# A recurrence and an MLP on one core: another string for the order of all steps

## The chip, the cores and the metric

The kernel runs on one core of one Trainium2 chip. A core has a matrix engine (TensorE, in profiles PE, with its weight loads as PEld), three engines for elementwise work (VectorE or DVE, ScalarE or ACT, GpSimd or POOL), and SyncE (SP), whose queue issues all of this kernel's DMA transfers in order. Every engine works through its own list of instructions in order, and waits with semaphores for the results of others. The metric is the time of one execution on the device in microseconds (us); it is given as the median of a few runs.

## The reference

Two blocks follow each other. The first is a recurrence with a complex decay; per batch and head (4 x 8), over 768 tokens, with states of 48 x 48:

```python
mag = np.sqrt(a_re * a_re + a_im * a_im)
scale = np.minimum(mag, 0.999) / (mag + 1e-06)
a_re_n, a_im_n = (a_re * scale, a_im * scale)
...
for t in range(S):
    ar, ai = (a_re_n[:, :, t, :, None], a_im_n[:, :, t, :, None])
    new_re = ar * S_re - ai * S_im
    new_im = ar * S_im + ai * S_re
    kv = np.einsum('bhd,bhe->bhde', k[:, :, t], v[:, :, t])
    S_re, S_im = (new_re + kv, new_im)
    y[:, :, t] = np.einsum('bhd,bhde->bhe', q[:, :, t], S_re)
```

Its output, laid out as 3072 tokens of 384 numbers, goes through an MLP with 2048 features:

```python
h = x @ w_in
g = np.maximum(h, 0.0) + alpha * np.minimum(h, 0.0)
return (g @ w_out).astype(np.float32)
```

The two weight arrays come in as 64-bit floats.

## The kernel before

The kernel is written as a set of Python generators ("tasks"). Each `yield` in a task ends a *step*; what stands behind a `yield` issues the instructions of that step, as a rule one to a few on one engine. A list of tasks is built, and a string decides which task makes its next step: one letter per step, 4292 letters in all.

```python
    def run(self, order):
        for c in order:
            next(self.tasks[self.LETTERS.index(c)], None)
```

So the string sets, for each engine and for SP's DMA queue, in which order the instructions of the tasks stand. Semaphore waits follow from the data. `Ring.put`, `takes=` and the numbers in the calls `DVE(...)`, `ACT(...)`, `PE(...)`, `DMA(...)` have no effect here: those calls return `None` and the body of `Ring.put` is `pass`. They are left from a planner that isn't part of the kernel.

The tasks and their letters:

- `A` to `I`, `gates`: the nine pieces of the decay, over one to three chunks of 128 tokens of a batch (`A`: batch 0, chunk 0; `B`: chunks 1 and 2; `C`: chunks 3 to 5; `D` to `I`: two halves for each of the other batches). A piece loads a_re and a_im (L248), makes magnitudes and phases on ACT and DVE (L253 to L311; the first DVE sum is L260), multiplies decays in a tree (L319) and writes them to the DRAM array `decs` (L324). It makes running products of phases with small products (L339, L341, on DVE where they are large, on POOL where they are small; in piece `A` all on DVE), carries them over the blocks (L379 to L414), and writes the phases to the DRAM array `phs` (L422, L432) after the products L427 and L430. The tile `gate` has two buffers, so a piece's loads wait for the end of the piece before the last.
- `J`, `loads`: per unit of 128 tokens the loads of queries and keys (tile `KQ`, L578, L580), phases (`PP`, L586) and decays (`T`, two transfers, L593).
- `K`, `half_rows`: copies rows of v to a DRAM array `vsc` (L561). `L`, `loads_v`: loads of v (`V`, L602 to L607, and `VL`, L625, L628).
- `M`, `pieces`: loads of `alpha` and of the 16 pieces of both weights (L492). `N` and `O`, `weights`: turn each piece into 32-bit floats in `to_f32` (L508, L510, L512 on ACT, L516 on POOL, L518 and L520 on DVE) for `w_in` and `w_out`.
- `P` to `Z` and `a` to `m`, `unit`: the 24 units (4 batches of 6 chunks) of the recurrence. A unit turns q and k by the phases (DVE L662, L664), then halves the distance of tokens level by level, 1 to 32: decay products on DVE (L718), copies on ACT (`WQ` L741, `W` L757), score products on PE (`ps_lv`, L679), masks on DVE or ACT (L703, L700). It then transposes k (PE L786, ACT L788, L789), makes the sum of the chunk's state (PE `ps_kv` L798, DVE `St` L827, L830, first set up with L723 and L726), the output (`ps_y`, PE L809, L818, L842), and stores it to DRAM (ACT L856, DMA L861). The state of a unit feeds the next unit of the batch.
- `n`, `loads_x`: loads the outputs of one or two units as `xT` (L874).
- `o`, `all_mlp`: the MLP over 14 groups of one or two units. A *feature* (16 in each group, 224 in all) is three products `ps_h` on PE (L890), a Relu on ACT (L897) and a DVE instruction (L899) that writes `g_sb`; then come the products `ps_o` of a unit with one feature (PE L909), 16 of them added up, a copy (ACT L919) and the store of 128 rows of the output (L922).

PE is needed by the units and by the MLP, and the MLP of a group can't start before its units have ended. DVE is needed by gates, weights, units and MLP.

Of the kernel before, what the change touches and what calls it, by code (L numbers as in the profile page):

```python
# [30 lines left out]
    "AAAAAAAAAAAAAAAAAAAAAAAAAAMMMAAMMJBBBBAMBJNNNNAAAAAAAAAAAAABABNANAAAAAABAAAABBABBNNAABBMBBABBNAAAABB"  # L31
    "BBBKBAAKKBJNABAKBAKAKAKAKOKNKJKKKKAAAAKOBBBANAABKABOMAABMAAAAABABAAABAAOOOOOOOBNNOOBBNOONNBNMNNNBJJB"
    "BBBBOPJPONPPPPPNMNPPOOPOOOPPCCLLMMMLLLLBLLJBCBBBPBBBBBBBJJBBBBBBBBBBBBBPPPPPPNOBCCCPCPPPBBNKCKKKKKCK"
    "LLKLBBBBBOBLLPPPPPPPPBBBBBBBPCCCCCLCBBNCCJBBBBPPPOBOOOOCPPPPBCMJDDCCNCCOCOCPCJCNCOOCJJJCOCONNNNCCCPD"
    "DKCQCCCCCDDNCLLLLCQDCCQCCCCCCCCCCCOQLNLPPPPPPMQMQQQQPPPPJQQLODDQQQODJJOJJJJJJQQQDDQCQCCDCCQDCQRKCOKL"
    "CLLLLLLKnRRRQRQRQQQQQQQQQQRQRQQRCCCCCQCQCRCNNNDDCDDoDQooDoooLLLoooQoDMoLQooCDDDCoRCoCoCDoooooNRoNNCo"
    "CoKNCCCCLLLRRRoooooLLLLLLDRLRRQQCCCCCCCRKKRMKCCRRoQCDooCQQQQRRoRRQCCoooooCoCoDDDRRRRRRRRRRoDoRJORoDR"
    "oDOOOOODRJJEJNDoooooLLDRRRRoRRRRDoSoOooSDSooDLoooJoLLooSSDSEoooSJooDooonoSSoDoSSDNNNSLLENoDoSSSoooLN"
    "DLooooSDooRSSSEJoJooOOoooooSSSoJLESoTESSSSLoLLLoTSJoooJSSSJooJSoJJooooSSSSSSooDESSEKTKESSESSSSSSDSoo"
    "UDUooTTTDoDTDoDDDDDDKooDDDDoooooooTDTTTLEoEToooELLTTTTTooooLoooJoJoTTooooEoUTTTTTTTTooooooUUTToUTTLT"  # L40
    "EELLLLLLLLDDDDDDEEEDDDDDDDDLoooDDDDDDoTooTTTTooTLnLLLEEoooEUULLLLLLLKoTooooooEoLUEoooLoToDDUoTDooDUo"
    "DDDDooooooooUEoEEUUoEEEDTToTTTTTooToUoUoUoooUooDUooooDooooUUUUUUUUUoooooDDDUoDooUoUUooooEUUUUUUoDoEo"
    "oEoEoooJUJUUUUUEUEJEEJJoooooEJEoEJooooEoEooEUooEooEoooooVoooooooJEoVooVoVoooooVFFJJJooooUVJVVVFoEEoE"
    "EooEoEEEEEEVEVEnooJJVVELEEEoooooooLVoWWVVooLoLoLLFFVoooVVoooVWoLoEoooLoEooVLoWEWWVWoVEoVVVVoEoWLWLWE"
    "WLooEoFLVVVEVLoooVJJoVEoooVEJEJJWEEEEEoEFVVVVVVoWWVVVWFFFooELELoEooWFFFFFoooooLoWWLLLLLLWLoEoooooLEo"
    "EEEEoEoELLLoWWVVVVVVVEWVWWooooEoEooooJJEJooWoXWWWEFJWWEooooooWWoooooWWWWWWWWXWLLLWWWWWWWXFFooWoLLooL"
    "LXXXXoXooooXXXoJJJooooGXooooLXoFFFoGXXXXooooLXXooFoFooFoXYXoFXGonooooJJooLLGoYXXXooooXXXoXXoFLoLLFFF"
    "FYFooFoXYFoXoGYYYFYXYooFFooJJooFYoYooooooFKoJooJXXXXYXXLXXXXXGXXXXooFoXFooooFGoGooFFFFFFFFFFJJFJYYYY"
    "FooooYooYYooZoZZZoFooLoFLLLLooLLFLLFGLooooLooYYYYYLYLYoZYZZZZoooooKKKYKYooYooYooJooFFYFGKFFGZGJJGYYY"
    "YYYYYYYYLooLLoLFGKGoYYYYYYoZoKZoKooooooJoFLoFLFGoFGFFFoFFoFFFFFFFFFFoLLLZZZZnLZZZLooLLKooooLFFooooZo"  # L50
    "FZZooFFZFZFFoFoFJJFoJooFoFFooZZZJZJZoFZooooZZooZZZZZZZZZZZZFLLLFoaZZZZZaoooooooooooJaJJooaoGoooaaaaa"
    "ooooaoooooaoooGaaaaaaaaoooobooooGJGooLGoGGJGGaaaaaaaJJaLLLaGoGoooGoLLLLbbbbHHooooooaoooLoabLooaGGooG"
    "aaaaaaGaGaGHbbbHbGbHKbKGJaJaaooooooGGboooooooaoaaaGGaGoJoobbbboooGbbGbGGGGoGGGbcoooooooooLooLobLLLbL"
    "LLHJLbLJLcbLbboobooocoHobooooHHHooocobbbooocccccobbooLcnooLooooJJJHbbHHHbobbbbooLoHLLLHGccLLoLLLLLGL"
    "LHoGoooHoGooJGooHGboooooGoocGccGcGbGGGGbbGcGcGcGoooobobbobGJoooGGGGooGGGccccGGGGcoocccooLdccocoooodc"
    "ococccccccccccbbooJJLLGGGGGGGJJJGJcodcHcLLGococcHGGGoGoGooooooooLLoLoLoodooooodHGGdHoGodddddKKooHLLL"
    "LoKooHoooodoooddddJodLHLHoHddooJooHooHooddHooonodddHdoodddddooooHHHHHHHooooddIIoooodHHoddddJdddJddLH"
    "JdHdedddHHddeJJJoJJJJJJHooooooooooeooHoooooeeeeeeHeoeooooofooeooooofeeoeffeooeoooLLoooooJeoeooooooLe"
    "oeeeeeeffooogHHHHHHfHHHHHHHHHHHHHfHHHHHHHgHeeeeLLLLLLLLLLIKoooooeooeefeeeeeeeKeeeeeKeeeeHHooHooooofo"
    "ooJoHHHHfHJLLoLfoLHHLLLLoooLLooLffJJffIoILofLoLfofooooogoooogfgffffgfggfoffooooogggIoffooooooHHHHHHo"  # L60
    "HoooofIKooHHooofffffKKfngfHHofggggIIooKKLooooLLLLLLggLLLLgoLHoooggggggggoffffoffffooHofggfgoooooooHo"
    "ooooJJogooooLoooooIIgoooIJIIIIJoJgJJgggggggggohooIggggoIIoooooooIohhoogLLLLJJhhJJJoohoooooohhoooIooh"
    "hooohohoooohooonohoioIohhhhhohooiihoooooooooooJohiihiooIihIhhhIIIIhLoohooooKhoooohhLLoLLLLLILLIoIIIh"
    "oooiiihihhhhhhhhhhhhhhhhLoLhioooIooooooLLLLLooioiiioooiioioooIoooooiJiiiJooJJJLJJIIIIIIooooojoIoIooo"
    "ooIooIooojjIIIoIIIIoLIIoIIoIiijiiiiioooooooLojjLoLLoioLooioiIIIIiIIIIIIiIIIIIiiILLjLLLLLLLLojjjoioiI"
    "iioooojojooooojjioiIooIIiIIIIoILoojjjjojoooiILjjojiiioLLIIIIIIIIoIioooonjjjjjjjjooooIooIIooIooIooIoo"
    "oojooooojjjjjjjjjjjjjjjJJJJJjooooooojoooooJJJJoooookkLkoooooookoJooooookkoookkoookkoLojokokoookkkkko"
# [34 lines left out]
def kernel(  # L102
# [83 lines left out]
    for h in (16, 32):  # L186
        by_row[h] = []
        for m in range(HC // h):
            t = next(column)
# [812 lines left out]
```

## Time and profile before

| what | value |
|---|---|
| time, median of 3 runs | 845.73 us (845.33 to 848.05) |
| span of the profiled execution (first to last instruction) | 837.2 us |
| time of the profiled execution beside its span | the page gives none; the median lies 8.5 us above the span |
| PE busy | 696.3 us (83%) |
| DVE busy | 648.1 us (77%) |
| ACT busy | 440.9 us (53%) |
| POOL busy | 245.1 us (29%) |
| moved by DMA | 130.91 MB, 156 GB/s in the mean |
| PE idle ahead of L890 / of L909 | 3.0 / 10.7 us |

How to read what follows. A span cut into slices shows each engine's busy share in tenths. A row of the waits names an instruction by engine, tile and line, what it waited for, the sum of those waits in us, how many there were, and the longest. A table of stretches gives for each stretch its length, then the busy time (and number of instructions) of PE, PEld, DVE, ACT and POOL, the clock granted to PE, the share of time in which the DMA engines were busy, and the GB/s they moved. Idle time of an engine costs nothing by itself; it counts where another engine waits for what comes late.

### The profile page before, as it was taken

How to read it: one execution, taken by the hardware profiler on the slowest of the kernel's cores; microseconds unless marked ns; L12 is line 12 of the kernel's file. 1: busy time of each engine (PE TensorE's matmuls, PEld its weight loads, DVE VectorE, ACT ScalarE, POOL GpSimd, SP SyncE). 2: the span in 40 equal slices, each digit the busy share in tenths (PEclk: the TensorE clock that was granted, in tenths of full speed). 3: DMA queues.
4: the chain of work that ended last, by engine and by line, in shares of the span. 5: the costliest groups of instructions: out<-in, count | busy, mean ns of one | idle time of the engine just before them, and what ended most of it. 6: DMA issues, size and time to landing. Idle time of an engine off the chain costs nothing.

```text
span 837.2 us, 26824 instructions
## 1 busy us (share of the span) xinstructions
PE 696.3 (83%) x11488; PEld 528.6 (63%) x11488; DVE 648.1 (77%) x953; ACT 440.9 (53%) x941; POOL 245.1 (29%) x352
## 2 busy tenths in 40 slices
PE   0002317768899999998999999999999999999998
PEld 0001316656777777776777777767777777777776
DVE  5988998989898998978998898796877856642112
ACT  7868876557645847473656544655443424232211
POOL 5376678817216400240134313500004300000000
PEclk9999757889999999999999999999999999999999
DMA  7695994696379468558854689457635493412100
GB/s 207 202 274 171 262 266 120 201 218 169 79 218 235 112 176 247 125 150 212 240 142 119 154 241 220 115 130 175 165 113 123 116 228 78 103 33 54 30 20 10
DMA packets 194174, 130.91 MB, mean 156 GB/s; under 512 B 74120, under 2 KB 185864, under 8 KB 194056
## 3 DMA queue, kind: packets, MB, share of 16 engines
q1 hardware_dynamic: 194056, 129.20, 58.7%
q8 instruction: 90, 1.47, 0.7%
q14 instruction: 28, 0.23, 0.1%
HBM read 100.82 MB, written 35.71 MB: 163 GB/s over the span
## 4 chain that ended last, share of the span: by engine, by line
PE 68%; DVE 12%; DMA 8%; ACT 5%; issue 3%; POOL 2%; SPq 2%; DVEq 0%; ACTq 0%; POOLq 0%
PE ps_h L890 27%; PE ps_o L909 26%; PE ps_lv L679 4%; PE ps_y L818 4%; DVE KQ L718 3%; PE ps_kv L798 3%; DMA T<-decs 3%; PE ps_y L842 2%; PE ps_kt L786 2%; DMA phs<-gate 2%; DVE gate L339 1%; DMA V<-in_v_dram 1%; DMA KQ<-in_k_dram 1%; DVE gate L341 1%; DMA St<-in_v_dram 1%
## 5 line engine op out<-in xcount | busy, mean ns | idle before, releaser
L890 PE MATMUL ps_h<-xT,w_in_sb 128*128 128x256 f32 (+1 forms) x1344 | 301.2, 356 | 3.0 <-issue 2.4
L909 PE MATMUL ps_o<-w_out_sb,g_sb 128*128 128x384 f32 x768 | 294.6, 497 | 10.7 <-DVE g_sb L899 8.3
L890 PEld LDWEIGHTS ps_h<-xT,w_in_sb 128*128 128x128 f32 x1344 | 234.1, 193 | 74.0 <-issue 4.3
L899 DVE SCALAR_TENSOR_TENSOR g_sb<-g_sb,al,ps_h 128x256 f32<-128x256 f32 (+1 forms) x224 | 97.5, 438 | 112.8 <-ACT g_sb L897 112.1
L909 PEld LDWEIGHTS ps_o<-w_out_sb,g_sb 128*128 128x128 f32 x768 | 137.7, 191 | 63.4 <-DVE g_sb L899 10.8
L718 DVE TENSOR_TENSOR KQ<-KQ,T 96x1024 f32<-96x1024 f32 x120 | 151.4, 1263 | 30.4 <-PE ps_lv L679 21.4
L897 ACT ACTIVATE g_sb<-ps_h 128x256 f32<-128x256 f32 (+1 forms) x224 | 78.7, 352 | 181.8 <-PE ps_h L890 181.1
L679 PE MATMUL ps_lv<-WQ 96*32 96x32 f32 x2304 | 34.5, 203 | 71.4 <-DVE WQ L662 55.1
L679 PEld LDWEIGHTS ps_lv<-WQ 96*32 96x32 f32 x2304 | 26.6, 115 | 93.1 <-DVE WQ L662 54.7
L339 POOL TENSOR_TENSOR gate<-gate 128x72 f32<-128x72 f32 (+1 forms) x56 | 40.0, 714 | 129.4 <-ACT gate L369 125.6
L741 ACT COPY WQ<-KQ 96x1024 f32<-96x1024 f32 x48 | 50.0, 1042 | 31.0 <-DVE KQ L718 30.7
L856 ACT COPY T<-ps_y 48x256 f32<-48x256 f32 x96 | 30.6, 365 | 46.8 <-PE ps_y L842 46.2
L757 ACT COPY W<-KQ 96x512 f32<-96x512 f32 x48 | 30.6, 638 | 45.7 <-DVE KQ L718 35.5
L516 POOL TENSOR_SCALAR top<-top 128x768 f32<-128x768 f32 x16 | 39.3, 2461 | 25.1 <-ACT top L508 17.1
L339 DVE TENSOR_TENSOR gate<-gate 128x576 f32<-128x576 f32 (+3 forms) x70 | 45.7, 653 | 1.2
L319 POOL TENSOR_TENSOR gate<-gate 128x72 f32<-128x72 f32 (+5 forms) x24 | 22.3, 929 | 76.6 <-DVE gate L319 74.3
L818 PE MATMUL ps_y<-A,VL 64*48 64x64 f32 x2304 | 43.5, 228 | 1.0 <-DMA VL<-vsc 0.7
L427 DVE TENSOR_TENSOR gate<-gate 128x1152 f32<-128x1152 f32 (+2 forms) x36 | 42.8, 1219 | 1.6 <-POOL gate L412 1.5
L679 PE MATMUL ps_lv<-KQ,W 96*32 96x32 f32 x1536 | 24.6, 205 | 23.4 <-ACT W L757 23.3
L818 PEld LDWEIGHTS ps_y<-A,VL 64*48 64x48 f32 x2304 | 41.6, 129 | 1.6 <-DMA VL<-vsc 0.9
L700 ACT ACTIVATE A<-ps_lv,columns 128x64 f32<-128x64 f32 x144 | 36.5, 334 | 9.6 <-PE ps_lv L679 9.5
L703 DVE TENSOR_TENSOR A<-ps_lv,mask 128x256 f32<-128x256 f32 x96 | 36.8, 412 | 0.0
(105 smaller groups left out, 925.3 us busy)
## 6 DMA issues: line engine op xcount, KB each, us to landing
T<-decs SPq DMA_DIRECT2D x48, 384.0 KB
PP<-phs SPq DMA_DIRECT2D x24, 387.0 KB
KQ<-in_q_dram SPq DMA_DIRECT2D x48, 192.0 KB
decs<-gate SPq DMA_DIRECT2D x7, 1152.0 KB
phs<-gate SPq DMA_DIRECT2D x14, 576.0 KB
KQ<-in_k_dram SPq DMA_DIRECT2D x40, 192.0 KB
vsc<-in_v_dram SPq DMA_DIRECT2D x48, 144.0 KB
VL<-vsc SPq DMA_DIRECT2D x24, 288.0 KB
```

The source lines that it names most:

```text
L339: on(4 * k).tensor_tensor(out=m, in0=w[:, 1::-1].unsqueeze(2).to_broadcast([P, 2, 2, k]), in1=pairs_of(u), op=ALU.mult)
L427: TT(out=m[:, a], in0=U5[:, 1 + a], in1=turned(off3, o)[:, a].unsqueeze(1).unsqueeze(3).to_broadcast([P, L // 2, nb, 2]), op=ALU.mult)
L516: nc.gpsimd.tensor_scalar(out=top, in0=top, scalar1=F64_SMALL, scalar2=None, op0=ALU.max)
L679: nc.tensor.matmul(t[64 * i + j:64 * i + j + HC // 2, p], lhsT=keys(n, g), rhs=queries(n, g), start=True, stop=True)
L703: nc.vector.tensor_tensor(out=a.rearrange("p n (g t) -> p n g t", g=2), in0=t.unsqueeze(2).to_broadcast(whole), in1=masks[name].rearrange( ...
L718: nc.vector.tensor_tensor(out=x, in0=x if x0 is None else x0, in1=m, op=ALU.mult)
L741: nc.scalar.copy(z.rearrange("p i n t -> p i (n t)").rearrange("p i (m h) -> p m i h", h=h), bass.AP(tensor=KQ.tensor, offset=KQ.offset + ...
L818: nc.tensor.matmul(o, lhsT=Vp[h][64 * i:64 * i + 64, s, e_ * D:(e_ + 1) * D], rhs=a, start=False, stop=False)
L890: nc.tensor.matmul(p, lhsT=w_in_sb[:, f // 2, kk, f % 2 * P:(f % 2 + 1) * P], rhs=x_of[m][:, kk], start=(kk == 0), stop=(kk == NK - 1))
L897: nc.scalar.activation(gt, p, AF.Relu, scale=-1.0)
L899: nc.vector.scalar_tensor_tensor(out=gt, in0=gt, scalar=al_1[:, f:f + 1], in1=p, op0=ALU.mult, op1=ALU.add)
L909: nc.tensor.matmul(sums[0], lhsT=gt[:, c * P:(c + 1) * P], rhs=w_out_sb[:, f], start=(f == 0), stop=(f == NF - 1))
```

## The change

The string `ORDER` is replaced by another one of the same length with the same count of each letter. In `to_f32` a call `R["top"].put(t)` is added after the last step's instruction.

```diff
@@ ORDER
 ORDER = (
-    "AAAAAAAAAAAAAAAAAAAAAAAAAAMMMAAMMJBBBBAMBJNNNNAAAAAAAAAAAAABABNANAAAAAABAAAABBABBNNAABBMBBABBNAAAABB"
-    "BBBKBAAKKBJNABAKBAKAKAKAKOKNKJKKKKAAAAKOBBBANAABKABOMAABMAAAAABABAAABAAOOOOOOOBNNOOBBNOONNBNMNNNBJJB"
...
-    "ommmoooooooooooonooooooooooooooooooooooooooooooooooooooooooooooooooooooooooooooooooooooooooooooooooo"
+    "AAAAAAAABAAAAAABAMBMMABAAMAMAKBAAAJAAAAKAABANBBAABKAJMAKAAKANJAAAAAKANBAAABAABAABAAAAOAJABBMAABMABNOAA"
+    "NABKKKBKAAAKOOBBAAAAAAABBBBABLABAKKABAMNAALABOOAANAAAABAANNAAAOBNANBNBNMBBNNOOOBLBBBBBNBBBBCCBCCBBBC"
...
+    "Loooommmommmooooooomoooooooooommooooooooommooomoooooooooomoooomoooomooooonoooooooooooooooooooooooooooo"
@@ to_f32
         nc.vector._custom_dve(ADD32_U16LIMBS, out=halfwords(dst), in0=halfwords(top), in1=halfwords(dst))
         slots.append(slot)
+        R["top"].put(t)
         return t
```

Each engine gets the same instructions as before, each with the same shapes and the same data. Their order changes on every engine. The longest run of steps that stand in the same order in both lists (with others in between) is 1126 of 1417 on PE, 499 of 937 on DVE, 483 of 888 on ACT, 306 of 322 on POOL and 434 of 731 transfers in SP's queue. On PE the units and the MLP alternate in nearly the same way: by the end of unit 8, for instance, 202 of the 672 `ps_h` products and 84 of the 384 `ps_o` products stand ahead before, 201 and 84 after. Most of the difference lies inside: the third piece of the gates (`C`) starts earlier and the first MLP products stand earlier, some copies of `half_rows` stand later, the last piece of the gates (`I`) starts earlier, and steps of different tasks alternate more often.

## The prediction

> **What bounds the kernel now.** I read the slices of the page first, then a table of stretches, then the waits of VectorE (DVE) and TensorE (PE), because the change moves instructions and adds none: the question is which engine is full at which time.
>
> ```profile
> PE   0002317768899999998999999999999999999998
> DVE  5988998989898998978998898796877856642112
> POOL 5376678817216400240134313500004300000000
> PEclk9999757889999999999999999999999999999999
> DMA  7695994696379468558854689457635493412100
> ```
>
> PE is idle for three slices, limps for eight, and is full from the twelfth (about 230 us) to the end. DVE is the other way round: full from the second slice to about the 28th (580 us). The table of stretches, cut where the feature counts below need it, gives the same in microseconds; its columns are busy time of PE, PE's weight loads, DVE, ACT and POOL, then the granted clock, the DMA share and GB/s:
>
> ```profile
> 8.00:57.00 49.00, 0.66 (x32) 0.52 (x32) 43.68 (x105) 37.27 (x56) 23.47 (x27) 1.00 0.80 225
> 57.00:221.00 164.00, 89.62 (x2104) 72.43 (x2108) 149.38 (x192) 112.58 (x205) 102.47 (x106) 0.82 0.73 197
> 221.00:261.00 40.00, 39.76 (x570) 31.32 (x559) 37.70 (x61) 18.70 (x48) 11.77 (x19) 1.00 0.75 207
> 261.00:578.00 317.00, 311.76 (x5410) 233.99 (x5409) 277.87 (x376) 179.08 (x399) 83.38 (x145) 1.00 0.65 169
> 578.00:837.00 259.00, 254.45 (x3392) 190.29 (x3390) 138.66 (x218) 88.84 (x232) 17.36 (x38) 1.00 0.37 94
> ```
>
> So there are two stages. Up to 221 us DVE bounds (149.4 of 164 us busy in the second row) and PE waits for it. From 221 us PE bounds: 606.0 of 616.2 us busy (sum of the last three rows). What the first stage wastes is in DVE's waits between 57 and 221 us:
>
> ```profile
> DVE g_sb L899 <- ACT g_sb L897: 3.2, 4, 1.0
> DVE KQ L718 <- DMA T<-decs: 2.4, 2, 1.9
> DVE KQ L718 <- ACT top L508: 1.7, 1, 1.7
> DVE WQ L662 <- DMA V<-in_v_dram: 1.7, 1, 1.7
> DVE KQ L718 <- ACT WQ L741: 1.4, 4, 0.5
> DVE gate L427 <- POOL gate L412: 0.8, 1, 0.8
> ```
>
> With the smaller rows of that answer they are 13.2 us: that is all that a better order can take out there. In the second stage PE hardly waits for anybody (221 to 838 us):
>
> ```profile
> PE ps_h L890 <- issue: 2.4, 2, 1.3
> PE ps_o L909 <- issue: 2.2, 1, 2.2
> PE ps_y L818 <- DMA VL<-vsc: 0.7, 1, 0.7
> ```
>
> A new order can gain 6 us there at the very most, and can lose much more.
>
> **The change, part by part.** The call `R["top"].put(t)` runs a method whose body is `pass`: no instruction, nothing. The rest is the order. Every step issues the same instructions as before, so no duration changes; what changes is what stands ahead of what. I therefore counted, in both lists of instructions, the DVE work that stands ahead of a landmark: each instruction taken with the time that it added to DVE's busy time in this profile. PE work is counted by the mean durations after 250 us, where the clock is full (0.45 us for the two passes of a 256-column `ps_h` product, 0.67 us for the two of `ps_o`, and so on). The landmarks are MLP features (one `all_mlp` feature is three `ps_h` products, one Relu on ACT, one L899 on DVE), numbered from 0 to 223:
>
> ```
> feature  its L899 ended   DVE work before/after   PE work before/after
>    0        137.6 us        117.5 / 107.3            13.2 /   8.5
>   24        221.0           193.1 / 184.3            60.8 /  59.4
>   42        261.0           230.7 / 229.5           102.4 / 102.4
>   60        318.2           284.8 / 286.7           159.6 / 159.6
>  100        462.8           412.2 / 421.1           299.7 / 300.5
>  132        578.4           509.0 / 523.2           412.8 / 411.4
>  148        636.5           556.2 / 555.4           467.8 / 467.1
>  212        818.4           643.4 / 643.4           653.4 / 653.4
> ```
>
> The new order is the old plan with its details moved: at features 42, 60, 148 and 212 both engines have the same work behind them. So the time is decided by how fast feature 42 is reached, and whether PE is held up between 42 and 132.
>
> *First, features 24 to 42.* Feature 24 has 8.8 us less DVE work ahead of it (193.1 - 184.3). With the same DVE waits it comes at 212.2 us. From there DVE needs 45.2 us of work to feature 42 and PE 43.0. At the DVE density of 220 to 240 us (19.64 of 20 us busy, 0.98) that is 46.1 us: feature 42 at 258.3 us in place of 261.0, a gain of 2.7 us. At the 0.943 of the whole old stretch (37.70 of 40, where PE held DVE back) the gain is 0.9 us; with DVE full it is 3.6. I take -2.7, because DVE is the slower of the two now.
>
> *Second, DVE's waits up to 221 us.* Three stand in places that the order moves. The second T load of unit 3 has 0.89 MB less ahead of it in SP's queue (36.26 to 35.37 MB; 4.5 us at the 197 GB/s of that row), and unit 5's first products (L718) have 8.7 us more DVE work ahead while their T load has the same bytes ahead: the 2.4 us for T go. Unit 3's PP load has 1.03 MB less ahead, and its V load (L602, L604) 0.5 MB less: 1.7 us at L662 go. The Abs of `top` on ACT (L508) that ends unit 0's 1.7 us at L718 moves from just behind that unit's W copy to 26 ACT steps later, and this L718 gets 4.5 us more DVE work ahead: it goes. That is 5.8 us. What is new: the third gate chunk's loads move up, from behind PP, T and St of unit 0 in SP's queue to ahead of them (position 44 to 38), and its first DVE sum (L260) from 52.1 us of DVE work to 41.2, ahead of unit 0's second product (L664). Its 1.18 MB end at 10.09 MB in the queue; the old queue had moved 10.34 MB when PP landed, at 51.8 us, so they land about 51 us; ACT's L253 to L258 take 1.4 + 1.05 + 1.05 us, so the sum can start at about 54.5 us; DVE gets there at 41.2 plus the 11.5 us that it lags its work at that point (unit 0 starts at 51.8 us with 40.0 us done), 52.7. That is 1.8 us of new wait, with unit 0 queued behind it. The net is -4.0 us; the ends are -13.2 (all waits go) and +13.2 (as many come back elsewhere). I stay at what I can name.
>
> SP's transfers of the first unit come 0.15 MB (PP) and 0.59 MB (its second T) later by the same count, 0.7 and 2.6 us at 225 GB/s; St landed at 55.8 us and made DVE wait until then anyway, and DVE has 1.4 us more work ahead of the first L718, so I set this at nothing; uncovered it costs 1.2 us. The copies of V's rows (`half_rows`, L561) move down by up to 11 MB, off the loaded stretch; their unit comes after 170 us. On POOL 306 of its 322 steps keep their order; it made DVE wait 1.1 us before 221 us, and I leave that. SP gets 22 more separate waits; at the 17 ns that one took on ACT that is 0.4 us beside SP's own long waits, so nothing.
>
> *Third, features 42 to 132.* By feature 132 the new order has put 293.7 us of DVE work where the old one had 278.3, in the same 317.4 us of PE time: the gate work of the last chunk moves up by 44.6 us of DVE work, and the units of that stretch end with 6 to 22 us more ahead of them. DVE must be 0.925 busy or PE waits. The old order ran it at 0.877 there, held back by PE (of its waits the largest are for PE and for ACT behind PE). The nearest rows for what DVE can do are 55.85 of 59 us (261 to 320 us, 0.947: no loss) and 149.38 of 164 us (57 to 221 us, 0.911: 322.4 us, a loss of 5.0). I take the middle, +2.5; the ends are 0 and, at 0.877, +17.5. The work comes back by feature 148, but time that PE lost doesn't.
>
> *Last*, from feature 148 on the counts agree within 4 us on PE and DVE has slack: 0.
>
> Sum: -2.7 - 4.0 + 2.5 = -4.2 us on the profiled span of 837.2 us. The median of the runs, 845.7 us, lies 8.5 us above that span (the page has no total of its own); I carry the 8.5 over: 841.5 us.
>
> **The clock.** The PEclk row drops to 0.5 between 100 and 120 us, where PE was busy for 2.62 of 20 us, and stands at 1.00 from 220 us. PE was busy for 90.3 us before 221 us with work worth 60.8 at full clock, so 29.5 us went to the slow clock and its small products. I give it nothing, since DVE was the full engine then and waited only 3.6 us for PE or for ACT behind it. [...]
>
> **The rivals.**
> - *The first stage closes up.* All 13.2 us of DVE's waits go, since the gates come earlier and the MLP starts with 10 us less DVE work ahead of it: -2.7 - 13.2 + 2.5, so 832.3 us. For it: DVE and PE both have their work sooner. Against: 4.6 us of the waits are for ACT results that the same chains need in any order.
> - *DVE becomes the bound between features 42 and 132*, and it ends slower. Halfway between 0.877 and 0.90 of density, 0.888, DVE needs 330.7 us, PE loses 13.3 us: -6.7 + 13.3 = +6.6, so 852.3 us; at 0.877 it is 856.5. It decides from a density of 0.906 down, where the loss eats the 6.7 us. For it: no stretch of 300 us ran denser than 0.911. Against: the old density there was held down by PE.
> - *Nothing comes of it.* The waits that go come back as others and only -2.7 + 2.5 remain: 845.5 us.
>
> **How the numbers follow.** A measurement here tells about 0.3% (2.5 us) from no change. The forecast has 0.42, by itself 836 to 848 us, and of it 0.31 lies below 843.2, 0.09 inside 843.2 to 848.3 and 0.02 above. The closed first stage has 0.15, all faster. DVE as the bound has 0.30, all slower. Nothing has 0.13: 0.04 faster, 0.05 same, 0.04 slower. So 0.50 faster, 0.14 same, 0.36 slower. The range goes from 829 (the sum's low end, -3.6 - 13.2 + 0 = -16.8 us, is 828.9) to 858 (just past DVE at its old density); an order with new waits all over, up to -0.9 + 13.2 + 17.5 or 875 us, stays out.
>
> **What the profile would show.** If the steps are right: feature 42's L899 ends near 254 us in place of 261; the waits of L718 for T and of L662 for V before 221 us are gone; a wait of about 2 us stands at the third gate's L260 near 53 us; DVE's density between feature 42 and feature 132 is 0.91 to 0.95; and PE waits for L899 or for KQ a few us there. Wrong: PE waits of more than 7 us for DVE behind 260 us (the slower rival), a first MLP product after 137 us, or SP stuck on one wait with unit loads behind it.

## The result and the profile after

The changed kernel takes 851.15 us (median of 8 runs, 847.27 to 856.83) where the kernel before, run beside it, takes 844.9 (841.79 to 848.05). The ratio is 1.0083, 95% interval 1.0055 to 1.0111: slower by 0.8%. The forecast was 841.5 us, faster.

Executions of one kernel differ by some 10 us here: the profiled one of before (span 837.2 us) was among its quickest, that of after (span 855.1, 856.83 us with what lies around it) was the slowest of its eight, and the ratios below leave out two executions in a slower state (1097.13 us of h1_new_head, 858.10 us of the repeat of the changed kernel). Around the span lie 1.7 us, not 8.5. A second profile of the changed kernel, taken in a later experiment, has a span of 844.7 us, 846.45 us in all, below its median there. What both profiles of the changed kernel show is what I go by.

The slices of the changed kernel, to be laid against those of before; TensorE (PE), VectorE (DVE), GpSimd (POOL), PE's clock and the DMA engines:

```profile
PE   0001327669999998997999998999999999999998
DVE  5989988999998989699689986998655765534112
POOL 5369596353505710274078022413211000000000
PEclk9999857899999989999899999999999999999999
DMA  7695994787686469547566795486455474411110
```

PE has dips in slices 16, 19 and 25 (321 to 342, 385 to 406 and 513 to 534 us) where before had nines but for one 8 in slice 19. PEclk shows an 8 in slices 15 and 20 (299 to 321 and 406 to 428 us). The table of stretches has the same cuts and columns as before (busy time of PE, its weight loads, DVE, ACT, POOL; clock, DMA share, GB/s):

```profile
8.00:57.00 49.00, 0.66 (x32) 0.52 (x32) 42.21 (x103) 36.06 (x55) 22.78 (x30) 1.00 0.76 217
57.00:221.00 164.00, 88.85 (x1991) 69.78 (x1992) 151.39 (x198) 114.07 (x204) 104.94 (x109) 0.86 0.74 197
221.00:261.00 40.00, 37.64 (x673) 28.64 (x672) 37.07 (x57) 19.58 (x50) 5.09 (x5) 1.00 0.82 219
261.00:578.00 317.00, 301.64 (x5117) 224.89 (x5116) 275.65 (x370) 174.80 (x381) 121.21 (x156) 0.97 0.65 168
578.00:837.00 259.00, 258.64 (x3600) 194.44 (x3599) 136.50 (x213) 88.83 (x238) 18.16 (x34) 1.00 0.39 95
```

The first stage got better: DVE is 2.0 us busier from 57 to 221 us (151.39 for 149.38). The loss is in the fourth row: PE is busy for 301.64 of 317 us where it was 311.76, and at a clock of 0.97. DVE isn't full there either (275.65 of 317, 0.87). The ends of L899 (L900 in the changed kernel) say when, in us, before and then after: feature 24 221.0 and 212.3; 42 261.0 and 259.6; 60 318.2 and 323.3; 100 462.8 and 481.4; 132 578.4 and 595.9; 212 818.4 and 835.7. So 8.7 us were won by feature 24, nearly all were gone by 42, and between 42 and 100 another 20 went. From there on the two run in step.

The DVE waits between 57 and 221 us, the view in which I had found the head's gain:

```profile
DVE top L518 <- POOL top L516: 3.7, 1, 3.7
DVE g_sb L900 <- ACT g_sb L898: 3.1, 4, 1.4
DVE KQ L719 <- ACT WQ L742: 1.9, 1, 1.9
```

The waits for V (1.7) and for the Abs of `top` (1.7) are gone, that for T went from 2.4 to 0.7; a wait for POOL of 3.7 us is new. And here is what PE waited for between 221 and 838 us, the view that I had read as "hardly waits for anybody":

```profile
PE ps_y L819 <- issue: 12.6, 4, 4.3
PE ps_kt L787 <- ACT T L790: 4.4, 4, 2.9
```

Both are new. The second profile of the changed kernel has them too, the first one smaller, and a third that is 0.2 us in the first profile and 0.6 in before:

```profile
PE ps_y L819 <- issue: 4.9, 2, 3.5
PE ps_kt L787 <- ACT T L790: 4.5, 4, 2.9
PE ps_lv L680 <- ACT W L758: 2.8, 3, 1.3
```

**What "issue" is here.** "Issue" is a wait for nothing that the profile shows. The timeline of PE in the changed kernel at the second of the four, in the middle of unit 8's products `ps_y`:

```profile
337.43 1.25 PE L819 MATMUL ps_y<-A,VL 64*48 64x64 f32 x65
342.55 0.66 PE L819 MATMUL ps_y<-A,VL 64*48 64x64 f32 x31 [3.87 <-issue]
```

PE stops after 65 of 96 equal products whose operands are long there. I numbered PE's instructions (weight loads, products and waits, 23,212 records in this trace). The four stops stand at the numbers 5313, 8129, 10177 and 13761; the three stops of before (its rows L890 and L909 for issue) at 8129, 10177 and 16065. All of these are 193 more than a multiple of 256. The page's part on the DMA queues has a line that fits (packets, MB, share):

```profile
q8 instruction: 90, 1.47, 0.7%
```

90 packets for 23,212 instructions is one packet of 16.4 KB for 256. In the trace such a packet lands at 341.16, 404.54 and 516.17 us, and PE goes on at 342.55, 406.06 and 517.58, that is 1.4 to 1.5 us later. So PE's instructions come by DMA in blocks of 256 here, and PE stands still when a block is late, for up to 4.3 us a time in this trace.

An estimate from the packets that aren't waited for: a block is asked for about 294 instructions ahead of its first use (with a lead of 280 some would have landed up to 0.7 us before they were asked for). Half of the packets land within 2.9 us of that point in before and 3.0 in the changed kernel, the latest 7 to 9 us after it. In the changed kernel the DMA engines were busy for 0.84 of the time or more while each of the eight that took over 7 us was on its way; in before one took 9.1 us at a share of 0.27, so load isn't the only reason. An MLP feature's 20 instructions take 2.6 us, so 294 of those last far longer. A unit's own products are a burst: 331 instructions in a row, weight loads included, took 2.4 us, and 8129 lies in or right behind such a burst in both kernels. At the stops at 8129, 10177 and 13761 PE was at the border 4.7, 5.1 and 7.1 us after that point, and the block landed 7.2, 7.9 and 8.4 us after it. So whether a block is late depends on how the burst lies against the multiples of 256, and on how long the packet takes at that moment.

Long stops cost twice here. In the changed kernel's trace the clock stands at 0.5 for 6.8 us from 299.4, 3.4 from 343.8, 6.8 from 405.2 and 3.4 from 517.9 us, each time at the end of or behind a wait of some 2.7 us or more; before has no half clock between 221 us and its last products. Behind a 256-column `ps_h` product the next one starts after 427 ns in these pieces and after 216 ns elsewhere (medians behind 221 us). The shortest wait that went with half clock was 2.73 us in this trace, 1.75 in a later run (a_gate); the one of 1.74 us at 5313 in this trace went without.

**The other wait.** The chain that ends at 300.1 us in the changed kernel (start, length, what):

```profile
289.52 4.97 POOL gate L400
...
297.81 0.04 ACTq L789
...
300.08 0.90 PE ps_kt L787 x4
```

POOL's L400 of the fifth gate piece takes 4.97 us (4.96 in the second profile); the next product on POOL starts behind it, and ACT's L406 waits 2.9 us for POOL. The same instruction took much less in before; the rows of L400 in before and after, and the wait on ACT:

```profile
L400 POOL TENSOR_TENSOR gate<-gate 128x126 f32<-128x126 f32 x14 | 12.2, 870 | 1.1
L400 POOL TENSOR_TENSOR gate<-gate 128x126 f32<-128x126 f32 x14 | 23.4, 1671 | 1.0
ACT gate L406 <- POOL gate L400: 2.9, 1, 2.9
```

In ACT's queue the copy of k of unit 7 (L789, L790) stands behind L406, and PE waits 2.93 us for that copy and then runs 6.8 us at half clock.

### The profile page after: what moved, and what is told of

Read it like the earlier page. It is cut to its first block, busy times and chain, and to the rows that moved or that the text cites. A ratio compares the mean times of both kernels' runs of the same rounds, so it can differ in the third digit from the quotient of the medians.

```text
span 855.1 us, 26830 instructions
## 1 busy us (share of the span) xinstructions
PE 701.5 (82%) x11488; PEld 528.7 (62%) x11488; DVE 647.1 (76%) x953; ACT 441.0 (52%) x941; POOL 278.9 (33%) x352
## 4 chain that ended last, share of the span: by engine, by line
PE 61%; DVE 14%; POOL 7%; DMA 6%; ACT 5%; issue 4%; SPq 3%; DVEq 0%; ACTq 0%; POOLq 0%
PE ps_o L910 24%; PE ps_h L891 24%; PE ps_lv L680 4%; PE ps_y L819 3%; POOL gate L339 2%; PE ps_kv L799 2%; DMA PP<-phs 2%; DVE gate L427 2%; DVE KQ L719 2%; PE ps_y L843 2%; PE ps_kt L787 1%; DMA T<-decs 1%; DVE gate L339 1%; POOL run L341 1%; DVE gate L341 1%
## 5 line engine op out<-in xcount | busy, mean ns | idle before, releaser
L910 PE MATMUL ps_o<-w_out_sb,g_sb 128*128 128x384 f32 x768 | 299.8, 505 | 9.1 <-DVE g_sb L900 8.1
L891 PEld LDWEIGHTS ps_h<-xT,w_in_sb 128*128 128x128 f32 x1344 | 237.7, 196 | 74.1 <-issue 2.9
L900 DVE SCALAR_TENSOR_TENSOR g_sb<-g_sb,al,ps_h 128x256 f32<-128x256 f32 (+1 forms) x224 | 97.7, 437 | 140.7 <-ACT g_sb L898 140.4
L910 PEld LDWEIGHTS ps_o<-w_out_sb,g_sb 128*128 128x128 f32 x768 | 138.9, 194 | 62.2 <-DVE g_sb L900 10.2
L819 PEld LDWEIGHTS ps_y<-A,VL 64*48 64x48 f32 x2304 | 39.7, 123 | 19.5 <-issue 19.1
L339 POOL TENSOR_TENSOR gate<-run,runs 128x12 f32<-128x12 f32 x46 | 31.8, 692 | 60.1 <-ACT runs L369 57.1
L516 POOL TENSOR_SCALAR top<-top 128x768 f32<-128x768 f32 x16 | 37.0, 2316 | 34.9 <-ACT top L508 34.9
L758 ACT COPY W<-KQ 96x512 f32<-96x512 f32 x48 | 30.7, 639 | 27.9 <-DVE KQ L719 23.7
L427 DVE TENSOR_TENSOR gate<-gate 128x1152 f32<-128x1152 f32 (+2 forms) x36 | 44.8, 1272 | 0.1
L701 ACT ACTIVATE A<-ps_lv,columns 128x64 f32<-128x64 f32 x144 | 38.6, 332 | 12.1 <-PE ps_lv L680 11.8
L857 ACT COPY T<-ps_y 48x256 f32<-48x256 f32 x96 | 32.4, 364 | 17.9 <-PE ps_y L843 17.0
L787 PE MATMUL ps_kt<-ident,KQ 96*128 96x96 f32 x192 | 25.8, 259 | 18.3 <-ACT T L790 13.7
```

The source lines that it names most:

```text
L339: on(4 * k).tensor_tensor(out=m, in0=w[:, 1::-1].unsqueeze(2).to_broadcast([P, 2, 2, k]), in1=pairs_of(u), op=ALU.mult)
L427: TT(out=m[:, a], in0=U5[:, 1 + a], in1=turned(off3, o)[:, a].unsqueeze(1).unsqueeze(3).to_broadcast([P, L // 2, nb, 2]), op=ALU.mult)
L516: nc.gpsimd.tensor_scalar(out=top, in0=top, scalar1=F64_SMALL, scalar2=None, op0=ALU.max)
L701: nc.scalar.activation(a[:, :, cols], t[:, :, at:at + name], AF.Copy, scale=s)
L819: nc.tensor.matmul(o, lhsT=Vp[h][64 * i:64 * i + 64, s, e_ * D:(e_ + 1) * D], rhs=a, start=False, stop=False)
L891: nc.tensor.matmul(p, lhsT=w_in_sb[:, f // 2, kk, f % 2 * P:(f % 2 + 1) * P], rhs=x_of[m][:, kk], start=(kk == 0), stop=(kk == NK - 1))
```

## The experiments

All but the last two compute the same thing as the kernels above. Ratios are to the kernel before, run beside each on the same chip; before took 842 to 844 us in these. Units are numbered 0 to 23 (letters `P` to `Z`, `a` to `m`), and `X34` is the step 34 of the task `X`.

A sum used throughout, of each profile: PE's gaps of over 0.25 us after 221 us, the time at half clock after 221 us (its end left out), the end of feature 42, and the span.

```
                     PE gaps   half clock   feature 42   span
before                  6.0        0.0         261.0     837.2
after                  17.1       20.5         259.6     855.1
after, once more       13.4        6.8         257.4     844.7
h1_new_head            10.9        3.4         256.8     839.5
h2_new_tail            13.7        3.4         260.1     845.8
a_fetch                15.0        3.4         258.8     844.3
a_both                 15.3        0.0         258.2     843.9
b_fetch                 6.5       10.2         260.3     841.1
```

The difference of two spans is close to that of the gaps, half of that of the half clock, and that of feature 42: for after 11.1 + 10.2 - 1.4 = 19.9, measured 17.9; for h2_new_tail 7.7 + 1.7 - 0.9 = 8.5, measured 8.6. So the loss is in PE's stops and slow products. Its make-up differs between the two profiles of the changed kernel. Against before, issue stops add 8.0 us in the first and 0.7 in the second (before has 4.6 of its own), waits for the copies T and W on ACT 4.0 and 6.7 (2.9 of them the chain above), and half clock 10.2 and 3.4.

**Which half of the order?** Two hybrids, cut at feature 42:

```diff
 ORDER =
-(all of the new string)
+(h1_new_head) new string up to feature 42, then the other letters in the old order
+(h2_new_tail) old string up to feature 42, then the other letters in the new order
```

> The new order up to feature 42 of the MLP, and the old order for all steps that are left (the two sets of steps differ there by ten). Both theories: the head alone is what the prediction's first two terms were about; in the new profile features 24 to 40 came 7 to 10 us earlier and feature 44 1.6 us earlier, so 2 to 6 us faster than before, about 841 us. If the head is what costs, this is slower than before.

> The old order up to feature 42, the new one behind it. Both theories put the loss there: between features 44 and 100 the new profile lost 20 us in its slow execution. So 7 to 15 us slower than before, 852 to 860 us. Theory of the fetch (PE runs dry because the next block of 256 instructions lands late behind data transfers): PE waits that no semaphore ends, of 2 to 4 us, right ahead of PE instructions whose number is 193 modulo 256, as in the new profile, and half clock behind them. Theory of late results (DVE and POOL work that was moved ahead): waits of PE that end with ACT or DVE.

h1_new_head took 841.97 us, ratio 0.9994 (0.9974 to 1.0015); h2_new_tail 851.75 us, 1.0101 (1.0061 to 1.0140). The whole loss lies in the new tail. The head's gain is real (feature 42 at 256.8 us) but gone by feature 60 (318.6, before 318.2). PE's waits after 221 us in h2_new_tail, one row, then in h1_new_head, two:

```profile
PE ps_y L818 <- issue: 7.0, 5, 3.5
```

```profile
PE ps_lv L679 <- ACT W L757: 3.3, 4, 1.3
PE ps_h L890 <- issue: 3.0, 2, 1.6
```

In the hybrid with the old tail the issue stops are again at 193 above a multiple of 256 (6593, 10177, 16065).

**Do the blocks decide?** If they do, instructions that do nothing, put in front, shift every later instruction against the blocks:

```diff
+        pad = ps.tile([P, HP, D2], F32, tag="misc", name="ps_pad")
+        for i in range(64):
+            nc.tensor.transpose(pad[:D2, 0], ident[:D2, :D2], ident[:D2, :D2])
```

They run in the first microseconds, when PE has nothing to do. 64 transposes are 128 instructions.

> The kernel before with 64 extra transposes of a constant ahead of everything on PE (128 more PE instructions; PE is idle there until 53 us), so that every block of 256 instructions begins 128 instructions earlier in the work. Theory of the fetch: in the old trace 12 block borders of 81 then lie behind 294 instructions that PE ran in 2.0 to 3.0 us, where none did before, and a block takes 2.9 us in the median and up to 8 us from its request; so about ten stalls of 1 to 5 us with half clock behind some of them, 10 to 30 us slower. Theory of late results: no change, within 2 us.

> The new kernel with the same 128 extra PE instructions. Theory of the fetch: the stalls of the new profile (units 5, 8, 10 and 14) go, and up to 12 others come where the 294 instructions ahead of a border took 1.9 to 3.7 us; 5 to 25 us slower than the new kernel, 856 to 876 us. Theory of late results: as the new kernel, 849 to 853 us, with the stalls in the same places of the order.

The old order became 886.46 us, ratio 1.0480 (1.0434 to 1.0526), more than the 10 to 30 us that I expected; the new one 859.48, 1.0193 (1.0164 to 1.0222). PE's waits after 221 us in the padded kernel before:

```profile
PE ps_y L818 <- issue: 20.3, 9, 5.1
PE ps_lv L679 <- issue: 5.8, 3, 2.7
```

All of the 16 issue stops stand at 193 above a multiple of 256, most of them at other products than before, and the clock is at half for 41 us around and behind them. Nothing else was changed, so the place of the blocks alone moves this kernel by 5%. I then chose a pad of 113 transposes from the bursts of the two orders, to make the place kinder:

> The kernel before with 113 extra transposes of a constant ahead of everything on PE (226 more PE instructions). In the old trace this puts the fewest block borders behind dense runs of small products. Theory of the fetch: the three waits of 1.3, 2.2 and 1.1 us go and hardly any come: 1 to 6 us faster than before, 838 to 843 us. Theory that 128 extra instructions did harm by themselves: slower again, by 10 us or more.

> The new order up to feature 42 and the old one behind it, with the same 226 extra PE instructions. Theory of the fetch: the head's 4 us, which this mix gave back in two late blocks and the half clock behind one, stay; 4 to 10 us faster than before, 834 to 840 us. If the head's gain is given back by results that DVE or a DMA brings late, 840 to 845 us.

Both missed: 852.22 us, 1.0099 (1.0065 to 1.0132), and 854.47, 1.0121 (1.0084 to 1.0159). Other blocks came late (14017, 15041 and 11201 with 3.1, 2.0 and 1.5 us in the first, 14017 and 6593 with 3.6 and 2.5 us in the second), and some 4 us of each loss stood at feature 42 already (264.6 and 260.8 us, without the pad 261.0 and 256.8), which I didn't follow up. 226 more instructions cost the old order less than 128, so it isn't their number that costs. Both pads made the old order worse, so its own place is one of the kinder ones; and the numbers of the instructions alone don't tell a good place, since the time that a block takes varies too (by the estimate above, from 1.3 to 9.1 us in before).

**Mend the late blocks of the changed kernel.** The MLP steps that stood ahead of a burst go into it, between the request and the need:

```diff
 unit 5:   -o248..o252 ahead of U34    +behind U34
 unit 8:   -o406..o413 ahead of X34    +behind X34
 unit 10:  -o522..o528 ahead of Z34    +behind Z34
 unit 14:  -o738..o744 ahead of d34    +behind d34
```

> The new kernel with 2 to 2.7 us of MLP products (steps of the letter o) put from ahead of the state products of units 5, 8, 10 and 14 to behind the second output step of the same unit, so that they stand between the request and the need of the four blocks that came late; nothing else moves and the instruction numbers stay. Theory of the fetch: the waits of 1.7, 3.9, 4.3 and 2.7 us ahead of the third and fourth output steps shrink below 2 us and the half clock behind them goes; in the median 3 to 9 us faster than the new kernel, 842 to 848 us. Theory of late results: the products wait as long for DVE as before, 850 to 854 us.

847.15 us, 1.0051 (1.0030 to 1.0072). The issue waits ahead of ps_y fell to 3.2 us (12.6 and 4.9 in the two profiles of the changed kernel), but PE's waits for the copies L789/L790 rose from 4.4 to 8.7: the products that I moved had covered them. The chain from POOL is another edit:

```diff
 fifth gate piece: -E82..E90 (L406 to L422) ahead of W29    +behind W31
```

> The new kernel with the ACT steps of the fifth gate piece that wait for POOL (L406 to L419, and what follows in that piece up to its phase stores) put from ahead of unit 7's transposed copies (L789, L790) to behind them. Theory that POOL's lateness counts through ACT's queue: the 2.9 us of PE ahead of unit 7's second transposes go, and up to 3.4 us of half clock behind them; 2 to 6 us faster than the new kernel, 845 to 849 us. Theory of the fetch alone: no change, 850 to 853 us.

849.51 us, 1.0072 (1.0042 to 1.0103): no clear change from the 1.0083 of the changed kernel. The 2.9 us wait is gone and one of 3.8 us stands at 314.6. The chain behind it in that run:

```profile
304.62 0.38 SPq L422
...
306.27 6.25 DMA T<-decs
```

The stores L422 now wait longer in SP's queue, and the T load of unit 8 stands behind them. So I moved only the three steps that matter, together with the blocks, and ran the changed kernel itself beside it:

```diff
 a_fetch, and
 fifth gate piece: -E82..E84 (L406 to L410) ahead of W29    +right behind W29
 unit 14:          -d35..d40 ahead of o745..o751            +behind o751
```

> The changed kernel once more, so that the next three stand beside it on the same chip. Both theories: about 851 us, 1.006 to 1.011 of the kernel before, with issue waits of PE ahead of ps_y of some 10 us behind 221 us, and a wait of about 3 us of ps_kt for ACT near 300 us.

> The changed kernel with both causes taken away that I name: the MLP steps that stand ahead of the bursts of units 5, 8, 10 and 14 go into them (as in the earlier version without the gate part; here five more MLP steps of one feature go into the burst of unit 14), and the three steps from L406 to L410 of the fifth gate piece stand behind the copy of k of unit 7 on ACT (L789), so that this copy no longer waits for POOL's L400. If late instruction blocks and the chain from POOL over ACT are the two causes: 840 to 845 us, ratio 0.997 to 1.002; the waits ahead of ps_y fall below 2 us, the 2.9 us wait of ps_kt near 299 us is gone and no half clock stands behind it. If the chain from POOL is a symptom of something else: 846 to 848 us, as with the first part alone.

The changed kernel took 848.64 us, 1.0068 (1.0038 to 1.0099), and a_both 845.84, 1.0028 (1.0007 to 1.0049). That is 2.8 of the 5.3 us that the change cost in this set; the two intervals overlap a little, so how much it is stays uncertain. Nothing runs at half clock between 221 us and the last products any more. What PE waits for then:

```profile
PE ps_kv L799 <- ACT T L790: 3.8, 4, 1.6
PE ps_kt L787 <- ACT T L790: 3.7, 4, 1.4
PE ps_lv L680 <- ACT W L758: 3.4, 5, 1.3
```

10.9 us in pieces of up to 1.6 us, all for copies on ACT (0.6 us in before, 7.3 in the second profile of the changed kernel), and issue waits of 3.1 us are left. My 840 to 845 us was missed, and the two causes aren't all; the moves also uncovered other waits, so this run doesn't give the price of the two causes by themselves.

**The same cure for the kernel before and for the hybrid.**

```diff
 both:         -X32 ahead of o414      +behind o423
               -Z42.. ahead of o522    +behind o537
               -g12.. ahead of o867    +behind o875   (unit 17; the expectation says 16)
 hybrid only:  -W12..W15 ahead of o318 +behind o325
```

> The kernel before with its own three late blocks mended: the products of unit 8 at L798 stand behind MLP feature steps up to 423 instead of ahead of 414, the end of unit 10 (from the second half of L842 on) behind step 537, and the first score products of unit 16 behind step 875, so that between the request for a block and its first instruction there stand 3 to 4 us more of MLP products. If PE's issue waits are late blocks: the three waits of 1.3, 2.2 and 1.1 us go, 4.7 us in all, 838 to 842 us, ratio 0.994 to 0.998. If they are something that goes with the steps around them: 842 to 848 us with issue waits at other numbers of instructions.

> The version with the new order up to feature 42 and the old one behind it, with the same three moves, and the first score products of unit 7 behind MLP step 325. That version's issue waits were 3.0 us ahead of ps_h and 2.9 ahead of ps_o, with 3.4 us of half clock behind one of them. If late blocks took back what the new head gained: the 5.9 us of waits and 1.7 us of slow products go, 834 to 838 us, ratio 0.989 to 0.995, faster than both kernels. If the gain is given back by DVE or ACT all the same: 840 to 844 us.

844.82 us, 1.0019 (0.9997 to 1.0042), and 846.07, 1.0029 (1.0003 to 1.0055). In b_fetch the issue waits did go, from 4.6 to 0.9 us, as blocks that are asked for in time should, if the estimated point of request is right. PE's waits after 221 us there:

```profile
PE ps_h L890 <- DVE g_sb L899: 2.1, 1, 2.1
PE ps_lv L679 <- ACT WQ L741: 1.5, 1, 1.5
PE ps_h L890 <- DMA xT<-ysc: 1.1, 1, 1.1
```

The products that I had put off were late for others, 10.2 us of half clock came behind that, and the kernel was no faster. In h1_fetch another block (5313) came late, and 17.1 us ran at half clock. A third try gave the bursts the MLP steps that come next, so that no product of a unit came later:

```diff
 a_pull:  seven next o-steps    -behind the burst    +behind U34, X34, Z34, d34
          -E82..E84, F20, H15 ahead of W29, W31, b31    +right behind them
 h1_pull: seven next o-steps    -behind the burst    +behind V36, Z34, f38
```

> The changed kernel with the blocks mended from the other side: behind the step 34 of units 5, 8, 10 and 14 the seven MLP steps that come next are pulled up into the burst, so that the MLP products between the two transposes of k and their copies on ACT (L789, L790) stay where they were. The steps from L406 to L410 of the fifth gate piece stand behind the first copy of k of unit 7, one L309 copy of the sixth piece behind its second, and L282 of the eighth behind that of unit 12. If the rest of the loss is PE's waits for ACT copies that the moves had uncovered or that stand behind gate work: the waits for L790 (7.5 us in the version with both causes mended) fall below 4 us and the time is 840 to 844 us, ratio 0.995 to 1.001. If it is DVE's density that makes the copies late: they stay, and the time is 845 to 848 us.

> The version with the new order up to feature 42 and the old one behind it, with seven MLP steps pulled up into each of the bursts of units 6, 10 and 16 (behind steps 36, 34 and 38), whose blocks came late; no product of a unit is moved. If late blocks took back the head's gain: no issue wait of over 1 us near instructions 6593, 10177 and 16065, 836 to 840 us, ratio 0.992 to 0.997, faster than both kernels. If the gain is given back by DVE or ACT all the same, or other blocks come late instead: 841 to 845 us, ratio 0.998 to 1.002.

845.70 us, 1.0027 (1.0003 to 1.0051), and 848.27, 1.0058 (1.0037 to 1.0080). In a_pull the waits for L790 fell from 7.5 to 1.3 us, and those for W (L758) rose from 3.4 to 5.3, with 1.2 for St and 0.7 for KQ new: the same time as a_both. h1_pull lost blocks at 7361 and 10177, and waits 3.4 us for g_sb and 3.0 for W.

**Is DVE short after all?** Cut finer than I had, the new order puts 57.2 us of DVE work into 57.2 us of PE work between features 42 and 60 (54.1 before), and 67.4 between 80 and 100 (60.8 before, in 68.5 us). In a_both these two stretches take 62.4 and 75.1 us. First I put the later gate pieces back to their old places:

```diff
 steps of the gate pieces F to I: -where the new order has them
                                  +behind the MLP step at which the old order has them, where that is later
```

> The version with both causes mended, with the steps of the last four gate pieces (F to I) put back, where they stood earlier, to the MLP step behind which the old order has them; TensorE's list of instructions is the same. The DVE work between features 42, 60, 80, 100, 116 and 132 goes from 57.2, 67.0, 67.4, 51.3, 50.8 us to 55.3, 64.9, 65.1, 52.4, 41.4. If DVE was short there: features 42 to 60 take 58 to 60 us in place of 62.4, 80 to 100 70 to 73 in place of 75.1, feature 132 comes 5 to 8 us after where it would by TensorE alone, and the time is 838 to 842 us, ratio 0.994 to 0.999. If the waits are for copies on ACT in any case: the stretches stay at 62 and 75 us, 845 to 847 us.

> The changed kernel with the same gate steps put back and nothing else: TensorE's list is that of the changed kernel, so its instruction blocks are cut where they were. If late blocks and the short DVE are two separate causes: about 3 to 4 us less than the changed kernel, 845 to 847 us, ratio 1.002 to 1.005, with issue waits ahead of ps_y as in the changed kernel (5 to 12 us). If the blocks come late because the gate pieces load the transfers: the issue waits go as well, 840 to 843 us.

914.89 us, 1.0856 (1.0825 to 1.0888), and 912.76, 1.0832 (1.0797 to 1.0866): no test of DVE at all. The stores of the gates moved with them, and SP, which issues its transfers in order, waits longer for them. A row of SP's waits in a_old_gates, 20.0 us in the changed kernel:

```profile
SPq L432 <- DVE gate L430: 33.1, 12, 7.0
```

PE's gaps there sum to 61.2 us. Then the clean way, which leaves every order as it is and takes DVE work away:

```diff
+        part = L // 4 if g >= 4 else L // 2
-                TT(out=m[:, a], in0=U5[:, 1 + a], ...
+                TT(out=m[:, a, 0:part], in0=U5[:, 1 + a, 0:part], ...
-            TT(out=by_place(p), in0=m[:, 0], in1=m[:, 1], op=ALU.add)
+            TT(out=by_place(p)[:, 0:part], in0=m[:, 0, 0:part], in1=m[:, 1, 0:part], op=ALU.add)
```

> The version with both causes mended, every instruction in its place, with the six products at L427 and L430 of each of the last five gate pieces done on half of their columns only (so half of these phases are left out): some 4 us less DVE work in each piece, one of them in each of the stretches between features 42, 60, 80, 100 and 132. If DVE is what is short there: features 42 to 60 take 58 to 60 us in place of 62.4, 80 to 100 71 to 73 in place of 75.1, and the time is 836 to 841 us, ratio 0.992 to 0.998. If the rest of the loss is copies that wait on ACT, or late blocks: 844 to 847 us, no change.

> The kernel before with the same products halved, as a control: there features 42 to 100 need 54.1, 66.6 and 60.8 us of DVE work in 57, 76 and 69 us and PE waits for DVE next to nothing behind feature 42. If DVE is short in the new order only: 841 to 844 us, ratio 0.997 to 1.002, and the lighter new order passes it by. If less DVE work shortens any order: 836 to 840 us, ratio 0.992 to 0.996.

b_light took 842.79 us, 1.0003 (0.9980 to 1.0026), as a control should. a_both_light took 846.42 us, 1.0042 (1.0015 to 1.0070): no faster than a_both. The two stretches did shorten as expected, to 60.0 and 72.4 us, but features 100 to 116 grew from 60.0 to 63.1 (a wait of 1.8 us for W ends at 478.6 us, and 3.4 us of half clock follow), and PE's waits stayed:

```profile
PE ps_kv L800 <- ACT T L791: 3.8, 4, 1.6
PE ps_kt L788 <- ACT T L791: 3.6, 4, 1.4
```

So what is left is not a lack of DVE time, as far as some 4 us a piece can tell. To see where PE loses, I counted PE's own work (each product by its mean duration at full clock in before, 662.8 us in all) and took the time at which so much of it was done, against the profile of before, in us:

```
PE work done    80    100    120    140    160    200    250    350    450    650
before       225.9  246.0  267.2  289.4  310.6  354.9  411.4  520.1  630.8  824.6
after         -6.2   -5.1   -0.9   -1.1   +4.9   +9.6  +15.0  +20.7  +17.2  +17.4
after_2       -6.8   -5.3   -2.7   -2.4   +2.4   +6.3   +6.0  +10.0   +7.1   +7.0
a_both        -8.0   -6.8   -2.3   -2.0   -0.5   +3.8   +2.0   +9.2   +6.4   +6.2
a_both_light  -7.9   -6.7   -2.3   -2.5   -1.0   +2.2   +1.4   +7.8   +4.9   +4.4
h1_new_head   -7.5   -5.9   -3.2   +0.2   +0.0   +0.3   +2.2   +1.7   +2.3   +2.3
h2_new_tail   -0.7   -1.0   -0.4   -0.2   +2.8   +6.9   +6.5  +10.9   +8.5   +8.5
```

PE's lead of 5 to 7 us shrinks by 2.6 to 4.5 between 246 and 267 us in every version with the new head, with either tail. (Steps of 1 to 2 us in this table can come from the mean durations and from another order of products within a stretch.) The step from 140 to 160 (+6.0 in after, +4.8 in its second profile) is the chain from POOL with its half clock, and a_both cuts it to +1.5. Those from 200 to 250 are late blocks in after (+5.4), not there in its second profile and in a_both. What no version with the new tail is rid of are the steps at 160 to 200 and 250 to 350.

## Why the prediction was wrong

- *Features 24 to 42, -2.7 us*: right. Feature 24 came at 212.3 and 211.8 us in the two profiles (212.2 by the DVE work alone), and from there to feature 42 it took 47.3 and 45.6 us (46.1).
- *The waits up to 221 us, net -4.0*: this came to nothing. The three named waits went, 5.1 us of the 5.8, and the new wait at the third gate's L260 didn't come. Two others did: L663 waits 3.0 us for PP ahead of 57 us (1.1 in the second profile, 0.5 before; I had set unit 0's later PP at nothing, covered by the wait for St, and that wait is gone), and L518 waits 3.7 us for POOL's L516, where I had left POOL aside. The waits between 57 and 221 us went from 13.2 to 10.4 and 11.9 us only, and by feature 24 nothing but the lesser DVE work had been gained: feature 42 came at 259.6 and 257.4 us, 1.4 and 3.6 earlier, where I had 6.7.
- *Features 42 to 132, +2.5*: this is the step that failed. The stretch took 336.3 us in the first and 327.9 in the second profile, for 317.4 before: +18.9 and +10.5. I priced it by DVE alone, and took PE's rows "<- issue" as a sum that can be gained at most. I had them in the view (2.4 and 2.2 us, three stops) and did not ask what they were. They are a price that a mere shift of PE's list changes: padding by 128 instructions made 35.8 us of them and the kernel 44 us slower. What took the place of my +2.5 is PE's own stops, late blocks and copies on ACT, with the half clock around them; only half of the loss is taken back by mending what I could name. My sentence that no duration changes was wrong too: POOL was busy for 245.1 us before and 278.9 after with the same 352 instructions, and one of them is the start of the chain over ACT.
- *The rest, 0*: right. From 450 us of PE work on, the lag stays at 17.2 to 17.4 us in the first profile and 7.0 to 7.1 in the second.
- *The 8.5 us around the span*: they are 1.7. The rest is the distance of that one execution from the median, so carrying the 8.5 over gave a sum near the median by accident.
- *The clock*: giving it nothing was right. Between 57 and 221 us it was 0.86 in one profile of the changed kernel and 0.98 in the other, and feature 24 came at 212.3 and 211.8 us. What I did not see is that it falls in the second stage (0.97 and 0.99 between 261 and 578 us).
- *The rivals*: DVE as the bound at 852.3 us is closest to the time, by luck and with the wrong cause. Its density came out (293.7 us of work in 336.3 and 327.9 us are 0.87 and 0.90), but not its sign: behind 260 us PE waits for DVE for 0 and 0.7 us in the two profiles, where I had set more than 7, and with less DVE work the mended kernel was no faster. The density I had forecast, 0.91 to 0.95, needed PE to run without stops, and nothing in my steps said why it should.

What is shown: the loss lies in the order behind feature 42 (h2_new_tail); PE's issue stops are late instruction blocks (numbers, landings, pads, and b_fetch, where they go when the request is given time, though the kernel doesn't get faster by it); mending late blocks and the chain from POOL over ACT takes back about half of the loss in the median (a_both; the intervals overlap a little). What stays open is the rest, some 2.5 us. In the traces it is PE's waits for ACT's copies of T and W in pieces of about a microsecond, partly uncovered by my moves; those for T stand in the new tail alone, those for W in the hybrid with the old tail too (3.3 us). It isn't DVE time (a_both_light); the moves that I tried only put it elsewhere. That these copies would be on time on another engine, or with more distance from their products, was not tried. No version beat the kernel before: h1_new_head, with the new head, is level with it.

## What to carry to other kernels

Where an engine issues tens of thousands of instructions and is full (23,212 on PE here), a wait "for issue" is worth a look before anything else: number the instructions, see if the stops share a remainder, as here 193 by 256, and treat every edit that moves the list, even a dummy in front, as one that may draw the blocks anew (128 instructions in front made the kernel before 4.8% slower). Here the blocks came late in or behind dense bursts of small products, and stops of some 2 us and more often brought 3.4 or 6.8 us of half clock (the one of 2.2 us in before did not). A cure that moves products to give a block time can uncover waits that those products had covered (4.4 us became 8.7 in a_fetch). An order that wins time in an early, DVE-bound stage has won nothing until the PE-bound stage behind it keeps it: follow the work of the engine that bounds the end, not the landmark of another.

## What the runs showed of the hardware that I had not expected

- Blocks of PE's instructions: all 62 issue stops of over 1 us behind 221 us in the twenty traces stand at 193 above a multiple of 256, and PE goes on 1.2 to 1.7 us after the packet lands. Half of the packets land within 2.9 us of the estimated point of request, the latest 7 to 9 us after it.
- 64 dummy transposes at the start, in idle time, made the kernel 4.8% slower, and 113 made it 1.0% slower.
- The same POOL instruction varies threefold: the 128x126 products at L400 took 870 ns in the mean before and 1671 after, and one of them 4.97 us; its twin 7 us later took 1.42, and DVE ran without a gap during both (287.67 to 298.78 us). What makes the difference no run here isolates.
